# Reloading the query weight a block of heads earlier in the backward pass of an attention decode kernel

## The chip, the cores and the metric

The kernel runs on one core of a Trainium2 chip. The metric is the device time of one execution in microseconds (us); smaller is better. Before the change seven runs gave a median of 1722.65 us (1720.59 to 1726.81).

A core has a matrix engine (TensorE, PE in the profile; its weight loads are PEld), a vector engine (VectorE, DVE), a scalar engine (ScalarE, ACT), GpSimd (POOL) and SyncE (SP), which here only issues transfers. Each engine runs its own instructions in order. A DMA is issued by one of these engines and then moves on 16 DMA engines; an instruction that waits for a DMA's semaphore holds up everything behind it on its engine.

## The reference

One decode step of a pre-norm transformer block and its vector-Jacobian product: the kernel returns the output and the gradients of all inputs.

```python
def _A_ref(x, k_cache, v_cache, wq, wo):          # B=4, Sq=1, D=512, H=32, Dh=128, Sk=4096
    q = (x @ wq).reshape(B, Sq, H, Dh).transpose(0, 2, 1, 3)
    scores = jnp.einsum("bhqd,bhkd->bhqk", q, k_cache) * (Dh ** -0.5)
    p = _softmax(scores, axis=-1)
    o = jnp.einsum("bhqk,bhkd->bhqd", p, v_cache)
    return o.transpose(0, 2, 1, 3).reshape(B, Sq, H * Dh) @ wo

h  = x + _A_ref(_layernorm(x), k_cache, v_cache, wq, wo)
h2 = h + _B_ref(_layernorm(h), w1, w3, w2)         # SwiGLU, F=1792
_out, _vjp = jax.vjp(_f, A_x, A_k_cache, A_v_cache, A_wq, A_wo, B_w1, B_w3, B_w2)
return (_out, *_vjp(grad_out))
```

All arrays are bf16. There are 4 x 32 = 128 heads (batch times head); each has a key and a value cache of 4096 x 128, 1 MiB apiece, and each cache has a gradient of the same size. So 128 MiB of keys and 128 MiB of values are read, the values a second time for the backward pass, and 256 MiB of gradients are written.

## The kernel before

**Two passes over the heads.** The forward pass takes the heads in pairs: it reads K and V, computes the softmax `P_all`, and keeps for each head a small matrix M (in eight slots of 16 heads) from which the gradient of the query is later formed. A middle part runs the feed-forward block forward and backward. The backward pass is the loop at L1175, one turn per head `s`:

- `prefetch` (L1168) or L1179 issues the load of the value cache of a later head (seven are held) from ACT (L793).
- `front(s + 1)` (L1140): TensorE transposes V of the next head in four groups (L760), ACT copies each back from PSUM (L761), TensorE forms `dP` with 32 small matmuls (L1148). Every fourth head `replicate` (L1126, L1129) first rebuilds the row copies `reps` that all of VectorE's products read.
- `grad_V(s + 1)`: VectorE writes the 1 MiB gradient of V into a slot `gv` (L766), POOL issues the store (L777).
- `grad_K(s)` (L1154): VectorE turns `dP` into `dS` (L1158, L1161) and writes the 1 MiB gradient of K into a slot `gk` (L766), SP issues the store (L1165).
- a turn of side work.

**Slots.** SBUF is cut into 23 slots of about 1 MiB. `Slot(...)` takes the slot that has been free longest, `give` puts it at the end of that queue. A slot is given back when its store has been issued; the next user of the same slot waits, by semaphore, for that store to have landed. So the length of the free queue is the number of stores that can be under way. Seven slots circulate among the value loads; the rest of the free ones carry `gv`, `gk` and the side work's tiles.

**Order of the DMAs.** The instruction streams show that each load and store issued from SP or ACT takes the next of eight semaphores in turn, and is issued only when the previous user of its semaphore has landed. With one value load and one `gk` store per head, a store waits for the `gk` store of four heads before, and a value load for the value load of four heads before. One more DMA on SP, a load of the side work, shifts this by one: for the four heads after it a value load waits for a `gk` store. POOL's stores have eight semaphores of their own.

**Side work.** `side_work` (L947) is a generator. The loop advances it by one step per head from head 21 and by three steps per head from head 59 (L1190). Its order is: 128 matmuls that form the gradient of the query from the M slots, three per step, which give back an M slot after each 16 (L952 to L957); the scaling into `dqT_bf` (L959 to L965); four small POOL transfers that lay it out as `dqflat` (L969); then the gradient with respect to the layernorm output, for which the query weight `A_wq` is read again in four slices of 1 MiB (`load_wq2`, L975, issued on SP at L977). For each slice `cc` TensorE transposes 32 blocks (L992), ACT copies them back (L994), and TensorE adds 32 matmuls (L997). After the four slices come the layernorm backward and the remaining weight gradients.

In the kernel before, slice 0 is asked for in step 46 of the side work (head 61) and first used in step 52 (head 63). Slices 1, 2 and 3 are asked for in steps 50, 59 and 68 and used in steps 61, 70 and 79.

Of the kernel before, what the change touches and what calls it, by code (L numbers as in the profile page):

```python
# [24 lines left out]
def kernel(  # L25
# [22 lines left out]
    nc = tc.nc  # L48
    P = nc.NUM_PARTITIONS
# [8 lines left out]
    HD = H * Dh  # L58
    assert NH == P and Dh == P and H == 32 and Sk == 32 * P
    assert D == 4 * P and F % P == 0  # L60
    DC = D // P
# [5 lines left out]
    MC = 16  # L67
# [107 lines left out]
    def ones_window(col):  # L175
# [11 lines left out]
                          in_=rowg[:, None, :, None].to_broadcast([P, 4, 8, 4]))  # L187
# [100 lines left out]
    def M_of(s):  # L288
        return Ms[s // MC].f(MC * (Dh + 1)).rearrange("p (n c) -> p n c", c=Dh + 1)[:, s % MC, :]
# [633 lines left out]
    with ExitStack() as c2:  # L923
# [23 lines left out]
        def side_work():  # L947
            pt = psg.tile([P, Dh], BF16, tag="gps", name="pt_O")
            nc.tensor.transpose(pt[:], OT_bf[:], ident_b[:])
            nc.scalar.copy(out=O_sb[:], in_=pt[:])  # L950
            dq_ps = psx.tile([P, 512], FP32, tag="x2", name="dq_ps")
            for s in range(NH):  # L952
                nc.tensor.matmul(dq_ps[:, s:s + 1], lhsT=M_of(s)[:, 0:Dh], rhs=dOT_f[:, s:s + 1], start=True, stop=True)
                if s % MC == MC - 1:
                    Ms[s // MC].give()
                if s % 3 == 2:
                    yield  # L957
            yield
# [11 lines left out]
            yield  # L970

            dx_ps = psx.tile([P, 512], FP32, tag="x2", name="dx_ps")
            wq2s = deque()

            def load_wq2(cc):  # L975
                wq2s.append(Slot("wq2"))
                nc.sync.dma_start(out=wq2s[-1].b(HD), in_=A_wq[cc * P:(cc + 1) * P, :])  # L977

            load_wq2(0)
            for _ in range(4):  # L980
                yield
            for cc in range(DC):
                if cc + 1 < DC:
                    load_wq2(cc + 1)
                yield
                yield
                wq2 = wq2s.popleft()
                wv = wq2.b(HD).rearrange("p (n c) -> p n c", c=P)
                for h0 in range(0, H, 8):
                    pt = psg.tile([P, 8, P], BF16, tag="gps", name="pt_wq")  # L990
                    for i in range(8):
                        nc.tensor.transpose(pt[:, i, :], wv[:, h0 + i, :], ident_b[:])  # L992
                    yield
                    nc.scalar.copy(out=wv[:, h0:h0 + 8, :], in_=pt[:])  # L994
                yield
                for h in range(H):
                    nc.tensor.matmul(dx_ps[0:B, cc * P:(cc + 1) * P], lhsT=dqT_bf[:, h * B:(h + 1) * B], rhs=wv[:, h, :],  # L997
                                     start=(h == 0), stop=(h == H - 1))
                    if h == H // 2 - 1:
                        yield  # L1000
                wq2.give()
                yield
            yield
            fs = Slot("fin")
# [55 lines left out]
            for i in range(2):  # L1060
                st = Slot("gw2")
                hw = hh_rows[:, i * 7 * P:(i + 1) * 7 * P].rearrange("b (p k) -> b k p", k=7)
                for k in range(7):
# [4 lines left out]
                                  in_=st.b(7 * D).rearrange("p (c j) -> p c j", c=7))  # L1068
# [4 lines left out]
            for (rows, out_ap) in ((dg_rows, out_6), (du_rows, out_7)):  # L1073
                for i in range(2):
                    st = Slot("gw13")
                    nw = hhat_bf[0:B, i * 2 * P:(i + 1) * 2 * P].rearrange("b (p k) -> b k p", k=2)
                    for k in range(2):
                        for (f0_, w_) in f_chunks:
# [5 lines left out]
                                      in_=st.b(2 * F).rearrange("p (c f) -> p c f", c=2))  # L1084
                    st.give()
            r1.give()
            for h0 in range(0, H, 8):
                st = Slot("gwo")
                ow = oflat.b(HD)[0:B, h0 * P:(h0 + 8) * P].rearrange("b (p k) -> b k p", k=8)
                for k in range(8):  # L1090
# [4 lines left out]
                                  in_=st.b(8 * D).rearrange("p (k j) -> p k j", k=8))  # L1095
                st.give()
            oflat.give()
            r2.give()

        units["s"] = side_work()  # L1100


# [121 lines left out]
```

## Time and profile before

| what | value |
|---|---|
| median of 7 runs | 1722.65 us |
| the profiled execution, its own time | 1722.65 us |
| its span, first to last instruction | 1720.3 us |
| bytes moved by DMA | 707.86 MB, mean 411 GB/s |
| HBM read, written | 422.59 MB, 282.34 MB |
| busy: TensorE, VectorE, ScalarE, GpSimd | 77%, 73%, 56%, 23% |
| one value load, one `gv` store, one `gk` store, issue to landing (median) | 15.2, 29.0, 22.4 us |
| a reload of the query weight, issue to landing (least, median, most) | 25.3, 29.5, 34.3 us |

The time between the span and the profiled execution's own time is 2.35 us. The profile cuts the span into 40 slices of 43 us; "DMA" is the mean busy share of the 16 DMA engines and "GB/s" what they moved. "idle before, releaser" stands for the time an engine sat idle just before an instruction, and what ended it. Where a stretch is asked for, each line gives the busy time of every engine in it, the granted clock of TensorE, the DMA share and the rate.

### The profile page before, as it was taken

To read this page: it belongs to the slowest core of one execution; us is meant where nothing else is said; L and a number is where in the kernel's file an instruction comes from. 1 tells how busy PE (TensorE), PEld (TensorE's weight loads), DVE (VectorE), ACT (ScalarE), POOL (GpSimd) and SP (SyncE) were. 2 spreads that over 40 slices of the span, in tenths; PEclk is the share of its full clock that TensorE was granted. 3 is DMA by queue.
4 is the path that set the end of the run, shared out by engine and by line. 5 is a ranking of instruction groups with operands and counts; after the bars stand their busy time and mean duration, and the time that the engine had idled before them with its cause. 6 is when DMAs were issued, how large, how long until landed. Compare 5 with 4: busy or idle time off the path is not lost. (4 is left out here: it accounts for less than half of the span.)

```text
span 1720.3 us, 44172 instructions
## 1 busy us (share of the span) xinstructions
PE 1329.8 (77%) x19124; PEld 1127.9 (66%) x19124; DVE 1253.1 (73%) x1389; ACT 960.2 (56%) x1470; POOL 401.8 (23%) x689
## 2 busy tenths in 40 slices
PE   5889888888888888887888787872777768777853
PEld 4767666676666666876778777762665556555652
DVE  5989899989998997666776766653667647555575
ACT  3455444444454444676655555552676657666752
POOL 1211222222222231231322211211223122212220
PEclk9999999999999999666555555565885565565555
DMA  9999999999999999999999999999999999999996
GB/s 397 418 419 418 419 418 419 418 419 419 413 416 408 419 404 390 381 420 423 422 422 423 423 422 423 422 422 405 371 423 412 425 426 405 404 422 422 421 422 286
DMA packets 101762, 707.86 MB, mean 411 GB/s; under 512 B 11052, under 2 KB 15288, under 8 KB 17600
## 3 DMA queue, kind: packets, MB, share of 16 engines
q1 hardware_dynamic: 63568, 432.04, 61.0%
q0 software_dynamic: 20864, 148.22, 20.6%
q10 hardware_dynamic: 17136, 124.79, 17.7%
q8 instruction: 150, 2.46, 0.6%
q14 instruction: 44, 0.36, 0.1%
HBM read 422.59 MB, written 282.34 MB: 410 GB/s over the span
## 5 line engine op out<-in xcount | busy, mean ns | idle before, releaser
L761 ACT COPY V<-pt_tps 128x1024 bf16<-128x1024 bf16 x512 | 492.8, 1016 | 200.2 <-PE pt_tps L760 178.5
L760 PE MATMUL pt_tps<-ident_b,V 128*128 128x128 bf16 x4096 | 453.5, 293 | 77.4 <-ACT V L761 73.6
L760 PEld LDWEIGHTS <-V 128*128 128x128 bf16 x4096 | 402.3, 138 | 142.2 <-issue 133.9
L766 DVE TENSOR_TENSOR gv<-P,reps 128x4096 bf16<-128x4096 bf16 x125 | 287.1, 2297 | 195.4 <-ACT reps L1129 83.6
L766 DVE TENSOR_TENSOR gk<-dS,reps 128x4096 bf16<-128x4096 bf16 x128 | 294.0, 2297 | 114.9 <-DMA out_dram<-gv 82.8
L433 PE MATMUL M_ps<-PK,Vn 128*128 128x130 bf16 x4096 | 285.2, 222 | 56.1 <-DMA Vn<-in_A_v_cache_dram 55.9
L418 DVE TENSOR_TENSOR PK<-Kn,PK 128x4096 bf16<-128x4096 bf16 x128 | 292.3, 2283 | 31.2 <-POOL PK L414 30.9
L433 PEld LDWEIGHTS <-Vn 128*128 128x128 bf16 x4096 | 251.6, 99 | 77.9 <-DMA Vn<-in_A_v_cache_dram 71.2
L325 DVE STREAM_TRANSPOSE KT<-Kn 128x512 f32<-128x512 f32 (+1 forms) x321 | 250.6, 797 | 0.3 <-issue 0.2
L320 ACT COPY KT<-pt_tps 128x1024 bf16<-128x1024 bf16 x128 | 129.5, 1012 | 197.0 <-PE pt_tps L319 152.0
L777 POOL DMA_DIRECT2D out_dram<-gv x128 | 68.3, 534 | 676.9 <-DVE dSt L1158 588.1
L1148 PE MATMUL dP_ps<-dOT_bf,V 128*128 128x1 bf16 x4096 | 151.0, 166 | 81.8 <-ACT V L761 61.4
L1148 PEld LDWEIGHTS <-V 128*128 128x128 bf16 x4096 | 140.3, 103 | 95.4 <-ACT V L761 72.9
L1138 POOL COPY P<-P_all 128x64 bf16<-128x64 bf16 x125 | 144.9, 1159 | 0.0
L331 POOL TENSOR_TENSOR W<-qrep,wmask 128x128 bf16<-128x128 bf16 x128 | 122.7, 958 | 83.7 <-PE S_ps L351 69.1
L414 POOL COPY PK<-P_all 128x64 bf16<-128x64 bf16 x128 | 32.6, 255 | 420.7 <-ACT P_all L408 417.6
L408 ACT COPY P_all<-pt_P 32x64 bf16<-32x64 bf16 x256 | 52.1, 203 | 58.4 <-PE pt_P L404 56.1
L1129 ACT CAST reps<-rep_ps 128x512 bf16<-128x512 f32 x62 | 36.4, 587 | 81.1 <-PE rep_ps L1126 47.0
L319 PE MATMUL pt_tps<-ident_b,Kn 128*128 128x128 bf16 x1024 | 80.8, 224 | 0.0
L443 PE MATMUL kP_ps<-PK,onesw 128*32 128x512 bf16 x1024 | 80.1, 389 | 0.0
L319 PEld LDWEIGHTS <-Kn 128*128 128x128 bf16 x1024 | 62.2, 100 | 25.9 <-issue 25.9
L351 PE MATMUL S_ps<-KT,W 128*32 128x256 bf16 x1536 | 75.5, 286 | 0.5 <-DVE KT L325 0.2
(239 smaller groups left out, 1283.4 us busy)
## 6 DMA issues: line engine op xcount, KB each, us to landing
Kn<-in_A_k_cache_dram SPq DMA_DIRECT2D x128, 1024.0 KB, 15.6
Vn<-in_A_v_cache_dram SPq DMA_DIRECT2D x128, 1024.0 KB, 16.2
out_dram<-gv POOLq DMA_DIRECT2D x128, 1024.0 KB, 29.0
out_dram<-gk SPq DMA_DIRECT2D x128, 1024.0 KB, 22.4
V<-in_A_v_cache_dram ACTq DMA_DIRECT2D x119, 1024.0 KB, 14.6
V<-in_A_v_cache_dram SPq DMA_DIRECT2D x9, 1024.0 KB, 19.0
wq<-in_A_wq_dram SPq DMA_DIRECT2D x8, 1024.0 KB, 18.2
out_dram<-gw POOLq DMA_DIRECT2D x6, 896.0 KB, 36.6
```

Of the source, the lines that this page charges most:

```text
L319: nc.tensor.transpose(pt[:, i, :], Kn[:, c * GW + i, :], ident_b[:])
L320: nc.scalar.copy(out=KT[:, c * GW:(c + 1) * GW, :], in_=pt[:])
L325: nc.vector.transpose(out=KT[:, c * w_:(c + n) * w_], in_=Kn[:, c * w_:(c + n) * w_])
L331: nc.gpsimd.tensor_tensor(out=W[:, hl], in0=qrep[:, :, s:s + 1].to_broadcast([P, 4, 32]), in1=wmask[:, hl, None, :].to_broadcast([P, 4, 32 ...
L418: nc.vector.tensor_tensor(out=PK[:, :, 0:Dh].rearrange("p j (r t) -> p j r t", t=2), in0=Ks[s].heads().rearrange("p j (r t) -> p j r t", t=2),
L433: nc.tensor.matmul(hold["M"][:], lhsT=Vn[:, j, :], rhs=PK[:, j, :], start=(j == 0), stop=(j == SJ - 1))
L443: nc.tensor.matmul(hold["kP"][32 * q:32 * (q + 1), :, :], lhsT=ones_window(w), rhs=PK[:, j0:j0 + 4, 0:Dh], start=(w == 0 and c == 0), stop ...
L760: nc.tensor.transpose(pt[:, i, :], v[:, g * GW + i, :], ident_b[:])
L761: nc.scalar.copy(out=v[:, g * GW:(g + 1) * GW, :], in_=pt[:])
L766: nc.vector.tensor_tensor(out=dst.rearrange("p j (r t) -> p j r t", t=2), in0=col2[:, :, None, :].to_broadcast([P, SJ, Dh // 2, 2]), in1=r ...
L1138: nc.gpsimd.tensor_copy(out=P2s[s][:], in_=P_all[:, s, :, None].to_broadcast([P, SJ, 2]))
L1148: nc.tensor.matmul(dP_ps[:, j:j + 1], lhsT=VT[:, j, :], rhs=dOT_bf[:, s:s + 1], start=True, stop=True)
```

## The change

The two definitions are moved ahead of the first loop of the side work. Slice 0 is asked for when the fourth M slot has been given back, and slice 1 when the sixth has. Slices 2 and 3 are asked for when the slice two before has been used up, one step earlier in the turn of the loop than before. The four empty steps ahead of the slices are gone.

```diff
+            wq2s = deque()
+
+            def load_wq2(cc):
+                wq2s.append(Slot("wq2"))
+                nc.sync.dma_start(out=wq2s[-1].b(HD), in_=A_wq[cc * P:(cc + 1) * P, :])
+
             dq_ps = psx.tile([P, 512], FP32, tag="x2", name="dq_ps")
             for s in range(NH):
                 nc.tensor.matmul(dq_ps[:, s:s + 1], lhsT=M_of(s)[:, 0:Dh], rhs=dOT_f[:, s:s + 1], start=True, stop=True)
                 if s % MC == MC - 1:
                     Ms[s // MC].give()
+                    if s // MC in (3, 5):
+                        load_wq2(s // MC // 5)
                 if s % 3 == 2:
                     yield
@@
             dx_ps = psx.tile([P, 512], FP32, tag="x2", name="dx_ps")
-            wq2s = deque()
-
-            def load_wq2(cc):
-                wq2s.append(Slot("wq2"))
-                nc.sync.dma_start(out=wq2s[-1].b(HD), in_=A_wq[cc * P:(cc + 1) * P, :])
-
-            load_wq2(0)
-            for _ in range(4):
-                yield
             for cc in range(DC):
-                if cc + 1 < DC:
-                    load_wq2(cc + 1)
                 yield
                 yield
                 wq2 = wq2s.popleft()
@@
                 wq2.give()
+                if cc + 2 < DC:
+                    load_wq2(cc + 2)
                 yield
```

After it the four slices are asked for in steps 22 (head 42), 32 (head 52), 54 (head 64) and 63 (head 67) of the side work, and used in steps 48, 57, 66 and 75 (heads 62, 65, 68 and 71). All side work behind them comes four steps sooner.

## The prediction

> **What bounds the kernel.** I read the two rows of rates in forty slices first, then the busy time of the engines in chosen stretches of the backward pass, then the instructions in order of time where the rate drops, and last the table of waits.
>
> ```profile
> DMA  9999999999999999999999999999999999999996
> GB/s 397 418 419 418 419 418 419 418 419 419 413 416 408 419 404 390 381 420 423 422 422 423 423 422 423 422 422 405 371 423 412 425 426 405 404 422 422 421 422 286
> ```
>
> The transfers bound it: no slice but the last is under 90% busy, and in the backward pass (slice 17 on) the rate stands at 422 GB/s. No compute engine is over 77%. So a change is worth what it does to the stretches below 422. The deepest are slices 27 and 28, 405 and 371, where the query weight is read again. Cut into stretches:
>
> ```profile
> 720.00:1165.00 445.00, 356.11 (x4499) 329.51 (x4500) 303.95 (x257) 266.36 (x293) 108.81 (x128) 0.56 1.01 421
> 1165.00:1195.00 30.00, 4.89 (x68) 4.39 (x67) 12.10 (x9) 5.03 (x6) 3.97 (x8) 0.56 1.01 418
> 1195.00:1220.00 25.00, 18.18 (x255) 16.78 (x256) 7.74 (x7) 15.13 (x16) 0.77 (x2) 0.69 0.86 331
> 1228.00:1236.00 8.00, 6.84 (x96) 6.42 (x95) 7.81 (x8) 5.58 (x6) 3.71 (x4) 0.71 1.00 341
> 1236.00:1295.00 59.00, 41.88 (x646) 37.23 (x644) 37.30 (x37) 39.74 (x45) 13.38 (x15) 0.82 1.01 424
> 1295.00:1305.00 10.00, 8.28 (x99) 5.70 (x95) 9.79 (x9) 7.65 (x12) 5.92 (x5) 0.50 0.99 372
> 1425.00:1435.00 10.00, 7.72 (x106) 5.42 (x105) 9.78 (x9) 8.32 (x12) 6.29 (x6) 0.67 0.99 356
> ```
>
> From 1165 to 1195 TensorE (first busy time) works 4.89 of 30 us, yet the rate holds at 418: queued transfers cover. Then they run out: 25 us at 331, share 0.86. Later dips, 8 to 10 us at 341 to 372, have a share near 1 and a VectorE (third time) that is busy almost without a break: it catches up after a wait. The instructions say why:
>
> ```profile
> 1171.97 0.33 ACTq L793 DMA_DIRECT2D V<-in_A_v_cache_dram  x1
> 1172.37 0.34 SPq L977 DMA_DIRECT2D wq<-in_A_wq_dram  x1
> 1172.40 0.59 ACT L1129 CAST reps<-rep_ps 128x512 bf16<-128x512 f32 x1 [11.68 <-DMA V<-in_A_v_cache_dram]
> 1173.04 0.58 PE L1126 MATMUL rep_ps<-qrows_bf,ident_b 128*128 128x128 bf16 x4 [11.44 <-ACT reps L1129]
> ...
> 1197.74 1.89 PE L992 MATMUL pt_wq<-ident_b,wq 128*128 128x128 bf16 x16 [18.83 <-DMA wq<-in_A_wq_dram]
> 1198.81 1.01 ACT L994 COPY wq<-pt_wq 128x1024 bf16<-128x1024 bf16 x1 [20.31 <-PE pt_wq L992]
> 1198.87 0.33 ACTq L793 DMA_DIRECT2D V<-in_A_v_cache_dram  x1
> ...
> 1205.00 0.25 DVE L1158 TENSOR_SCALAR dSt<-dP_ps,c_rep 128x32 f32<-128x32 f32 x1 [19.64 <-PE dP_ps L1148]
> ```
>
> Slice 0 is issued at 1172.37 and first used at 1197.74, 25.4 us later; TensorE stands 18.8 us at it. Behind it on TensorE are the transposes of the next V, behind those ACT's copies and the next value load, and VectorE gets no `dP` for 19.6 us. Just before, ACT had waited 11.68 us to issue a value load: the load of slice 0 had shifted the turn of the eight semaphores, and this value load waited for a `gk` store. The two waits in a row emptied the queue; the table of waits has the second once only:
>
> ```profile
> PEld L992 <- DMA wq<-in_A_wq_dram: 18.9, 1, 18.9
> PE pt_wq L992 <- DMA wq<-in_A_wq_dram: 18.8, 1, 18.8
> ```
>
> **The change part by part.** Durations are from the profiled execution; its own time, 1722.65 us, is the median, and 2.35 us lie outside its span.
>
> *Removed: the wait for slice 0.* Slice 0 goes out 19 `gk` stores sooner on SP (43 instead of 62 ahead of it), slice 1 ten sooner (53 instead of 63). In steady state SP issues a `gk` store every 7.8 us, so slice 0 has some 20 heads or 156 us until its use and slice 1 13 heads or 101 us, against landings of 25.3 to 34.3. Both will be there. The stretch 1195 to 1220 lost (422 - 331)/422 x 25 = 5.4 us: that is the gain if the queue no longer runs out. Its bounds are 5.4 and 0, the latter if another wait empties it. I take 5.4. The dip at 1228 to 1236, where VectorE catches up, lost (422 - 341)/422 x 8 = 1.5 us, and goes with the wait.
>
> *Moved: two loads on SP at heads 42 and 52.* No instruction is added: four loads of 0.34 us issue, the same bytes. What moves with each is the shift of the semaphores: for four heads value loads wait for `gk` stores, on ACT ahead of its copies, so TensorE and VectorE behind them are late. The nearest row is the 11.68 us above. From below it costs nothing: after the loads of slices 2 and 3 in the kernel before (1209.7 and 1232.9) VectorE waits up to 9.6 us for `reps`, yet 1236 to 1295 runs at 424; and 1165 to 1172, right behind the 11.68 us, still ran at 415 or more. From above each costs one catch-up dip, 1.5 us. I take nothing: both come with a full queue and no second wait near.
>
> *Two slots held longer.* From head 42 the free queue is one shorter, from 52 two: 10 to 13 instead of 11 to 15 up to head 61. It hides: at heads 19 to 26, with 6 or 7 free, slices 18 to 21 run at 422 to 423. I take 0; the upper bound is a further dip of 1.5.
>
> *Changed: slices 2 and 3.* They are used 12 steps after they are asked for, 4 heads, instead of 11. But before, the first wait had emptied the queue and SP ran right behind VectorE. Now the queue is full. SP issues `gk` of head 61 at 1164.8, 10 us after `front(62)` ended on TensorE at 1154.6. So the lead is 4 x 7.8 to 8.3 (with the weight's extra MiB) less 10, some 21 to 23 us, and TensorE would wait 2 to 13 us for each slice, less what the semaphore shift makes TensorE late anyhow. A wait of 11.4 us cost no rate above, one of 18.8 behind it did. Bounds: 0, and 5.4 + 1.5 = 6.9 each. I take one dip of 1.5 and 1.0 of a half-emptied queue, nearer the lower end since 2 to 13 is nearer to 11.4 than to 30.
>
> *Four steps sooner.* The later side work meets other heads. Its dips (1295: 1.2 us; 1425: 1.6 us) come from waits for particular slots and may move either way, 2.8 us at most; I take 0. The side work ends at head 111 instead of 112, far from the end, which is bound by stores; nothing comes of that.
>
> Sum: -5.4 - 1.5 + 1.5 + 1.0 = -4.4; 1722.65 - 4.4 = 1718.2 us.
>
> One rule speaks against so much. The Trainium skill, DMA: Bandwidth & Descriptors, section Specifications, gives a limit of about 358 GB/s for one core's share of HBM. If that were the ceiling, 331 GB/s would be a loss of only (358 - 331)/358 x 25 = 1.9 us and the dip at 341 of 0.4, and an estimate by that page would be 1722.65 - 1.9 - 0.4 + 2.5, about no change. The measured 421 GB/s over 445 us rules it out here, where one core runs, and I go by 422.
>
> **The rivals.**
>
> *The wait only moves.* Slices 2 and 3 keep about the landing of slice 0 and a full queue; if the shift (11.7 us) and the wait for the slice fall together for one of them as before, the queue empties there: +5.4 + 1.5 against -6.9, that is 1722.7, with 1720 to 1725. For it: a lead of 21 to 23 against landings up to 34.3. Against it: the shift makes TensorE late and so gives the load more time.
>
> *Slower: both slices empty it.* One mechanism, place heads 64 to 71: each of slices 2 and 3 comes with a wait like the 18.8 us. Price 2 x 6.9 - 6.9 = +6.9, 1729.6. It decides from where shift and wait add up to about 30 us twice; then the result is over 1726. Against it: after the first such wait SP no longer lags and the second load gets its 32 us, as slices 2 and 3 did before.
>
> *More.* The later dips also go: -5.4 - 1.5 - 0.5 (398 GB/s in 1172 to 1180) - 2.8 = -10.2, 1712.5.
>
> That the change doesn't do what it says can be left out: SP's stream shows the loads moved, and nothing ahead of them on SP waits for the side work.
>
> **How the numbers follow.** Forecast (1715 to 1720.5): 0.52. The wait only moves: 0.24. Both empty it: 0.16. More: 0.08. About 0.2%, 3.4 us, is what a measurement of this kernel can tell from no change: faster is below 1719.2, slower above 1726.1. Of the forecast's 0.52 I count 0.44 as faster and 0.08 as same; with the others faster is 0.52, same 0.32, slower 0.16. The range reaches from the most that can go, 1712.5, to the edge of the slower case, 1726.0; the forecast's own range is 1715 to 1720.5.
>
> **What would show it.** Right: no wait of the transposes L992 for slices 0 and 1; no stretch near head 62 with a DMA share under 0.95; rates of 420 to 424 around heads 42 and 52 in spite of an ACT wait of some 11 us at each; the loads of slices 2 and 3 with 20 us or more to landing. Wrong: a share under 0.9 in heads 64 to 72 (the wait moved), or a dip after head 42 or 52 (the shift is not hidden).

## The result

| | before | after |
|---|---|---|
| median | 1721.5 us (1719.8 to 1726.8, 59 executions) | 1725.6 us (1722.1 to 1728.3, 23 executions) |
| ratio to before, 95% interval | | 1.0018 (1.0013 to 1.0024) |
| span of the profiled execution | 1720.3 us | 1724.4 us |

The 1722.65 us that the prediction starts from is the median of the first seven of the 59. By the ratio the change costs 3.1 us (2.2 to 4.1). That is under the 0.2% that I had named as what a measurement can tell, and yet outside the interval: a very small loss where I had forecast a gain of 4.4 us.

In the kernel after, `load_wq2` issues on L955, the transposes of a slice are L989, ACT's copies of it L991, the `reps` copies L1128, their matmuls L1125. The first two rows of the page, after:

```profile
DMA  9999999999999999999999999999999999999996
GB/s 397 418 419 418 419 418 419 418 418 418 412 417 406 419 404 391 378 421 423 424 424 425 425 426 425 425 413 409 398 366 421 424 421 410 391 421 418 420 422 277
```

The two low slices before the change (405 and 371, slices 27 and 28, the first being 0) are four now: 413, 409, 398 and 366 in slices 26 to 29. The hole is wider, not filled, and the pair at slices 33 and 34 is a little deeper (410 and 391 against 405 and 404). The waits of TensorE for the slices, after:

```profile
PE pt_wq L989 <- DMA wq<-in_A_wq_dram: 2.5, 1, 2.5
```

The three numbers are us in total, times and the longest. 18.8 us have become 2.5. So the wait that the change removes is gone. What has come in its place is seen in the stretches, after (length, busy time of PE, PEld, DVE, ACT, POOL, granted clock, DMA share, GB/s):

```profile
1015.00:1060.00 45.00, 29.62 (x364) 27.84 (x364) 26.87 (x21) 21.61 (x24) 11.03 (x10) 0.54 1.01 425
1060.00:1110.00 50.00, 36.90 (x445) 34.75 (x445) 32.41 (x28) 24.29 (x26) 9.04 (x14) 0.53 1.01 426
1125.00:1135.00 10.00, 8.78 (x117) 8.39 (x115) 9.54 (x9) 5.44 (x6) 5.11 (x5) 0.50 0.98 376
1165.00:1175.00 10.00, 8.38 (x94) 7.75 (x95) 8.73 (x10) 6.05 (x7) 5.67 (x8) 0.50 0.96 359
1205.00:1235.00 30.00, 17.30 (x242) 15.43 (x242) 16.11 (x13) 15.76 (x18) 7.71 (x6) 0.73 0.98 384
1250.00:1290.00 40.00, 30.77 (x465) 26.51 (x463) 28.62 (x31) 29.47 (x35) 12.60 (x12) 0.83 0.95 361
1455.00:1515.00 60.00, 39.33 (x428) 29.99 (x427) 31.16 (x27) 34.10 (x47) 11.80 (x20) 0.53 0.99 391
```

Against 423 GB/s each row loses (423 - rate)/423 of its length: 1.1 and 1.5 us in the two dips at 1125 and 1165, 2.8 and 5.9 us where slices 2 and 3 are issued and used, 4.5 us in the later weight gradients. The kernel before loses 5.4, 1.5 and 1.2 at the query weight (the prediction's rows) and 2.0 in the last of these stretches, which runs there at

```profile
1455.00:1515.00 60.00, 42.93 (x488) 33.01 (x488) 34.63 (x28) 38.85 (x53) 14.54 (x21) 0.59 1.01 409
```

The instructions of ACT in order of time show the shift of the semaphores after each of the four loads on SP (issued at 1015.7, 1106.4, 1202.9 and 1224.9), after:

```profile
1023.03 0.59 ACT L1128 CAST reps<-rep_ps 128x512 bf16<-128x512 f32 x1 [17.38 <-DMA out_dram<-gk]
...
1114.20 1.93 ACT L761 COPY V<-pt_tps 128x1024 bf16<-128x1024 bf16 x2 [15.23 <-DMA out_dram<-gk]
...
1210.24 1.93 ACT L761 COPY V<-pt_tps 128x1024 bf16<-128x1024 bf16 x2 [7.50 <-DMA out_dram<-gk]
...
1240.39 1.93 ACT L761 COPY V<-pt_tps 128x1024 bf16<-128x1024 bf16 x2 [4.66 <-DMA out_dram<-gk]
```

Each time a value load stands in front of ACT's copies and waits for a `gk` store. VectorE, which makes all the stores, is late behind the last two:

```profile
1218.63 2.29 DVE L766 TENSOR_TENSOR gv<-P,reps 128x4096 bf16<-128x4096 bf16 x1 [15.78 <-ACT reps L1128]
...
1244.90 0.25 DVE L1157 TENSOR_SCALAR dSt<-dP_ps,c_rep 128x32 f32<-128x32 f32 x1 [8.94 <-PE dP_ps L1147]
...
1255.55 2.29 DVE L766 TENSOR_TENSOR gv<-P,reps 128x4096 bf16<-128x4096 bf16 x1 [7.82 <-ACT reps L1128]
```

15.8 us idle, and then 16.8 of some 20. A dip goes with each (1215 to 1235 and 1250 to 1270), and in five us of the second the share falls to 0.70:

```profile
1255.00:1260.00 5.00, 4.24 (x46) 4.01 (x46) 4.38 (x4) 3.87 (x5) 1.86 (x2) 0.53 0.70 282
```

### The profile page after: what moved, and what is told of

The parts are those of the page before. It is cut to its first block, busy times and chain, and to the rows that moved or that the text cites. A ratio compares the mean times of both kernels' runs of the same rounds, so it can differ in the third digit from the quotient of the medians.

```text
span 1724.4 us, 44171 instructions
## 1 busy us (share of the span) xinstructions
PE 1330.8 (77%) x19124; PEld 1129.6 (66%) x19124; DVE 1253.7 (73%) x1389; ACT 960.7 (56%) x1470; POOL 418.6 (24%) x689
## 4 chain that ended last, share of the span: by engine, by line
DMA 44%; DVE 7%; PE 5%; ACT 3%; issue 3%; POOL 0%; ACTq 0%; DVEq 0%; SPq 0%; POOLq 0%
DMA out_dram<-gk 21%; DMA out_dram<-gv 16%; DVE gv L766 3%; DMA wq<-in_A_wq_dram 3%; DMA out_dram<-gw 2%; DMA w2b<-in_B_w_dram 2%; ACT V L761 2%; DVE gk L766 2%; PE pt_tps L760 1%; PE M_ps L433 1%; DVE PK L418 1%; PE pt_w L562 0%; POOL P L1137 0%; PE o_ps L1051 0%; ACT Pn L397 0%
## 5 line engine op out<-in xcount | busy, mean ns | idle before, releaser
L761 ACT COPY V<-pt_tps 128x1024 bf16<-128x1024 bf16 x512 | 492.6, 1015 | 218.9 <-PE pt_tps L760 174.8
L1137 POOL COPY P<-P_all 128x64 bf16<-128x64 bf16 x125 | 160.7, 1286 | 0.0
L1128 ACT CAST reps<-rep_ps 128x512 bf16<-128x512 f32 x62 | 36.4, 586 | 79.6 <-PE rep_ps L1125 59.0
L397 ACT ACTIVATE Pn<-E,rl 128x1024 bf16<-128x1024 f32 x64 | 73.7, 1152 | 3.2 <-DVE rl L394 3.2
## 6 DMA issues: line engine op xcount, KB each, us to landing
Kn<-in_A_k_cache_dram SPq DMA_DIRECT2D x128, 1024.0 KB, 15.8
wq<-in_A_wq_dram SPq DMA_DIRECT2D x8, 1024.0 KB, 20.3
```

The lines of the kernel that those rows point to most:

```text
L761: nc.scalar.copy(out=v[:, g * GW:(g + 1) * GW, :], in_=pt[:])
L1137: nc.gpsimd.tensor_copy(out=P2s[s][:], in_=P_all[:, s, :, None].to_broadcast([P, SJ, 2]))
```

## The experiments

The first three theories: **A**, the shift of the semaphores that each lone load on SP brings is no longer hidden when two come near each other; **B**, the two slots held from heads 42 and 52 are missing; **C**, the later side work, four steps sooner, meets worse heads. **D**, that time not lost at the query weight is lost at the next late transfer, came with the first results; **E** and **F** are given where they came up.

For each run I cut the profiled execution into stretches of 5 us and add up (423 - rate)/423 x 5. "Heads 49 to 54" is 1100 to 1185 us, "query weight" 1185 to 1310, "row stage" 1340 to 1530 (the row copies, their matmuls and the weight gradients that follow); these three columns add up only the stretches under 412 GB/s, the column "700 to 1700" adds up all. The ratio is that of the measured times, to the kernel before on the same chip; the losses are those of one execution.

| run | median, us | ratio (95%) | heads 49-54 | query weight | row stage | 700 to 1700 | span |
|---|---|---|---|---|---|---|---|
| before | 1721.5 | | 0.4 | 8.1 | 3.8 | 17.4 | 1720.3 |
| after | 1725.6 | 1.0018 (1.0013-1.0024) | 2.6 | 8.4 | 4.8 | 20.4 | 1724.4 |
| 1 all from POOL | 1724.2 | 1.0012 (1.0003-1.0021) | 0.5 | 6.5 | 8.4 | 20.1 | 1723.7 |
| 2 in pairs | 1723.5 | 1.0006 (0.9997-1.0015) | 3.1 | 0.5 | 8.3 | 17.9 | 1720.8 |
| 3 slices 0, 1 from POOL | 1722.0 | 0.9998 (0.9989-1.0006) | 0.3 | 1.4 | 11.1 | 18.2 | 1721.3 |
| 4 slices 2, 3 from POOL | 1723.3 | 1.0007 (0.9998-1.0016) | 2.8 | 0.7 | 10.2 | 17.5 | 1721.0 |
| 5 empty steps back | 1722.5 | 1.0004 (0.9995-1.0013) | 1.5 | 9.2 | 1.5 | 17.3 | 1720.8 |
| 6 = 3 with 5 | 1721.1 | 0.9992 (0.9983-1.0001) | 0.0 | 0.2 | 9.8 | 15.4 | 1718.0 |
| 7 before, lone shifts | 1722.2 | 1.0003 (0.9994-1.0012) | 0.0 | 9.5 | 2.5 | 15.5 | 1719.5 |
| 8 before, slots held | 1722.9 | 1.0003 (0.9994-1.0012) | 0.5 | 8.3 | 1.9 | 17.2 | 1721.0 |
| 9 = 6, rows early | 1721.1 | 0.9996 (0.9987-1.0005) | 0.3 | 0.6 | 11.3 | 16.6 | 1719.0 |
| 10 = 9, oflat early | 1721.2 | 0.9995 (0.9986-1.0004) | 1.0 | 0.4 | 6.0 | 15.8 | 1719.1 |
| 11 before, rows early | 1722.9 | 1.0008 (0.9999-1.0016) | 0.0 | 10.1 | 2.0 | 19.6 | 1723.7 |
| 12 before, close shifts | 1723.0 | 1.0005 (0.9996-1.0013) | 0.0 | 7.6 | 3.5 | 18.1 | 1722.3 |
| 13 after, two steps | 1727.5 | 1.0030 (1.0018-1.0042) | 2.3 | 7.6 | 3.7 | 19.4 | 1723.7 |
| 14 after, four steps | 1722.7 | 1.0005 (0.9996-1.0014) | 1.9 | 7.7 | 7.5 | 21.9 | 1723.0 |
| 15 = 6, two steps at rows | 1721.2 | 0.9989 (0.9980-0.9998) | 0.0 | 0.2 | 12.5 | 16.7 | 1718.4 |
| 16 before, two steps | 1724.3 | 1.0014 (1.0005-1.0022) | 0.0 | 8.3 | 6.0 | 20.1 | 1725.6 |
| 17 = 9, row slots kept | 1722.5 | 1.0000 (0.9991-1.0009) | 0.5 | 1.1 | 11.2 | 17.4 | 1719.4 |
| 18 = 10, row slots kept | 1721.5 | 0.9997 (0.9988-1.0005) | 1.3 | 0.9 | 7.0 | 16.9 | 1720.1 |

Over these 20 executions the span rises by 1.09 us for each us of the column "700 to 1700" (correlation 0.89): the account of lost transfer explains most of the differences in span. The single columns do not stand for it (correlations 0.23, 0.65 and -0.39), and this is what the rest is about.

A rate under 423 is not the same as idle DMA engines. Between 1165 and 1530 us the engines' missing share, (1.01 - share) x 5 us over the same stretches, adds up to 4.9 us of the 12.4 lost before, 4.9 of 14.7 after and 6.4 of 10.0 in run 6. The rest is lost while the engines count as busy, as in 1455 to 1515 of the kernel after (391 GB/s at a share of 0.99); no run shows why.

### Where the slices are issued (1 to 4)

**1: all four slices from POOL**, whose stores have semaphores of their own, so that nothing shifts on SP and ACT.

```diff
-                nc.sync.dma_start(out=wq2s[-1].b(HD), in_=A_wq[cc * P:(cc + 1) * P, :])
+                nc.gpsimd.dma_start(out=wq2s[-1].b(HD), in_=A_wq[cc * P:(cc + 1) * P, :])
```

> The changed kernel with all four reloads issued from POOL instead of SP, at the same steps and into the same slots. POOL's stores have their own eight semaphores, so the turn of the eight that SP and ACT share is not shifted. Theory A, the shift of the turn is what costs: the ACT waits of 17.4 and 15.2 us for a gk store at heads 42 and 52 and the one of 7.5 us at head 65 go, the stretches below 400 GB/s between heads 52 and 72 go with them (1.1 + 1.5 + 2.7 + 5.8 = 11.1 us lost in the changed kernel), and the time falls to 1713 to 1719 us, below the kernel before (1721.5). Theory B, the two slots held early shorten the queue of stores: same slots, so the time stays at 1724 to 1727. Theory C, the later side work meets other heads four steps sooner: same steps, so it stays at 1724 to 1727.

Slower than before by 0.12%, and not in theory A's range. The dips at heads 49 to 54 are gone, but now one of the late slices is not there in time and TensorE waits 19.0 us for it, in this run's table of waits:

```profile
PE pt_wq L989 <- DMA wq<-in_A_wq_dram: 19.2, 2, 19.0
```

So this run trades the shift for the wait and does not tell them apart at slices 2 and 3.

**2: in pairs on SP**, slices 0 and 1 at head 36, 2 and 3 at head 52. Two loads in a row move the turn by two, and value loads wait for value loads again.

```diff
-                    if s // MC in (3, 5):
-                        load_wq2(s // MC // 5)
+                    if s // MC in (2, 5):
+                        load_wq2(2 * (s // MC == 5))
+                        load_wq2(2 * (s // MC == 5) + 1)
...
-                if cc + 2 < DC:
-                    load_wq2(cc + 2)
```

> The changed kernel with the four reloads still on SP but in two pairs: slices 0 and 1 when the third M slot is given back (head 36), slices 2 and 3 when the sixth is (head 52). A pair moves the turn of the eight semaphores by two, so value loads go on waiting for value loads and gk stores for gk stores. Four slots are held until use instead of two. Theory A (shift): no ACT wait for a gk store of over 5 us near heads 36, 52 and 64 to 68; time 1713 to 1719 us. Theory B (slots): four slots fewer hurt more than two, 1727 us or more. Theory C (steps): 1724 to 1727.

The query weight now loses 0.5 us instead of 8.4. But ACT waited 42.1 us for slices (two value loads had one ahead of them in the turn), heads 49 to 54 lose 3.1, and the row stage 8.3. The time is that of before within its interval, and in none of the three ranges.

**3 and 4: two slices from POOL, two from SP.**

```diff
+                (nc.gpsimd if cc < 2 else nc.sync).dma_start(out=wq2s[-1].b(HD), in_=A_wq[cc * P:(cc + 1) * P, :])
```

> The changed kernel with slices 0 and 1 issued from POOL and slices 2 and 3 from SP as they are: the shifts at heads 42 and 52 go, those at heads 64 and 67 stay. If the shifts at 42 and 52 carry the loss, the time falls to 1719 us or less. If those at 64 and 67, where 2.7 + 5.8 us are lost in the changed kernel, carry it, the time stays near 1723 to 1725.

```diff
+                (nc.sync if cc < 2 else nc.gpsimd).dma_start(out=wq2s[-1].b(HD), in_=A_wq[cc * P:(cc + 1) * P, :])
```

> The changed kernel with slices 2 and 3 issued from POOL and slices 0 and 1 from SP as they are: the shifts at heads 64 and 67 go, those at 42 and 52 stay. If the shifts at 64 and 67 carry the loss, the time falls by some 5 to 8 us, to 1717 to 1720. If those at 42 and 52 do, it stays at 1724 to 1726. By theory A the gains of this run and of the one with slices 0 and 1 on POOL add up to that of all four on POOL.

These two place the dips. With slices 0 and 1 on SP (run 4) the dips at 1125 and 1165 are there as in the kernel after; with these two on POOL (run 3) they are not. Stretches of run 4, then of run 3:

```profile
1125.00:1135.00 10.00, 8.78 (x116) 8.39 (x114) 9.54 (x9) 5.27 (x6) 5.11 (x5) 0.50 0.99 374
1165.00:1175.00 10.00, 8.38 (x95) 7.75 (x95) 8.99 (x10) 6.07 (x8) 5.80 (x8) 0.50 0.96 365
1205.00:1235.00 30.00, 21.70 (x344) 19.11 (x343) 19.73 (x16) 21.04 (x24) 6.63 (x9) 0.84 1.01 423
...
1385.00:1410.00 25.00, 12.77 (x144) 8.73 (x142) 19.10 (x17) 9.18 (x11) 8.58 (x8) 0.64 0.86 322
```

```profile
1125.00:1135.00 10.00, 7.59 (x86) 7.04 (x85) 7.37 (x6) 5.03 (x6) 2.96 (x3) 0.50 1.00 421
1165.00:1175.00 10.00, 8.05 (x127) 7.40 (x125) 6.93 (x5) 7.08 (x8) 3.88 (x6) 0.67 1.01 407
1205.00:1235.00 30.00, 20.67 (x279) 18.56 (x278) 16.12 (x14) 17.49 (x20) 9.28 (x9) 0.72 1.01 421
```

So the 2.6 us at heads 49 to 54 come from the early loads on SP. The 8.4 us at the query weight fall to 0.7 when the late pair leaves SP, and to 1.4 when the early pair does: it takes all four, one by one, to lose them. And both runs lose 10 to 11 us at the row stage, where the kernels before and after lose 4 to 5; run 4's 25 us at 322 GB/s are a hole that neither of those has. This is where theory D comes from. In time, neither run is in a range that was given for it, but both are faster than the kernel after (1.0018): run 3 by 0.0020, plus or minus 0.0010, or 3.4 us, and run 4 by 0.0011, plus or minus 0.0011, or 1.9 us, just at its bound (the half widths of the two intervals added in squares, here and below). So the early pair on SP costs time in the kernel after; without it the time is that of the kernel before, and no better.

### The four steps, alone and together with POOL (5 and 6)

```diff
+            for _ in range(4):
+                yield
```

> The changed kernel with the four empty steps put back ahead of the slices: the loads of slices 0 and 1 stay early on SP, but slices are used in steps 52, 61, 70 and 79 as in the kernel before, and all later side work meets the same heads as before. Theory C (the side work four steps sooner is what costs after head 72): the loss behind 1300 us falls from 5.2 us in the changed kernel to the 5.0 of the kernel before or less and the time is 1 to 3 us below the changed kernel's 1725.6. Theory A (shift of the turn): the shifts at heads 42, 52, 65 and 68 all stay, 1724 to 1726. Theory D (the queue of transfers that reaches the later side work full loses there what was won earlier, wherever its steps fall): 1721 to 1725, with the loss behind 1300 us larger than before.

The changed kernel with the four empty steps ahead of the slices is as fast as the kernel before within its interval: 1.0004. Against the kernel after (1.0018) that is 0.0014 or 2.4 us, plus or minus 1.8 by the two intervals (0.00055 and 0.0009 added in squares). So C holds in part. The place is the later stretch, 1455 to 1515, at 411 GB/s here against 391:

```profile
1455.00:1515.00 60.00, 41.54 (x512) 32.94 (x509) 35.69 (x29) 39.82 (x54) 15.53 (x21) 0.66 1.01 411
```

At the query weight this run loses 9.2 us, no less than the kernel after, although its table of waits has no wait of TensorE for a slice at all.

Run 6 has both: slices 0 and 1 from POOL as in run 3, and the four steps.

> Slices 0 and 1 early from POOL (no shift at heads 42 and 52, as in the run with slices 0 and 1 on POOL, which lost only 1.7 us up to 1300 but 11.1 us behind it), and the four empty steps put back. Theory C: behind 1300 us the loss is that of the kernel before, 5.0 us, so the time is some 6 us below that run's 1722.0: 1715 to 1718. Theory D: behind 1300 us it loses 9 to 11 us again in spite of the old steps, 1720 to 1723.

Its stretches show a query weight that costs nothing, and a row stage that does:

```profile
1165.00:1205.00 40.00, 28.37 (x420) 26.32 (x421) 28.79 (x24) 25.45 (x29) 11.77 (x14) 0.69 1.01 420
1205.00:1290.00 85.00, 59.83 (x854) 53.41 (x854) 55.84 (x53) 53.60 (x62) 21.86 (x25) 0.72 1.01 421
1290.00:1380.00 90.00, 68.28 (x776) 53.86 (x775) 47.76 (x40) 62.80 (x82) 19.07 (x24) 0.58 1.01 423
1385.00:1435.00 50.00, 31.55 (x350) 22.54 (x350) 33.60 (x30) 26.08 (x34) 17.07 (x18) 0.60 0.88 341
```

In 1205 to 1290, where the kernels before and after lose most of their 8 us, it runs at 421. It reaches the row stage at 423, and then loses (423 - 341)/423 x 50 = 9.7 us in one place. Its instructions there:

```profile
1375.19 0.53 POOL L1033 DMA_DIRECT2D rows<-in_grad_out_dram  x1
1384.46 0.60 POOL L1034 CAST rows<-reps 4x512 bf16<-4x512 f32 x1 [8.73 <-DMA out_dram<-gv]
```

```profile
1412.18 1.01 PE L942 MATMUL gps<-rows 4*128 4x512 bf16 x2 [11.02 <-DMA rows<-in_grad_out_dram]
```

A load of 4 KB, the rows of the output gradient, takes 36.9 us from issue to landing behind the stores on POOL's queue, and TensorE stands 11 us at it. And POOL's first write into the slot of the rows waits 8.7 us for the store that was in that slot. The kernel before has no such wait at the row slots, the kernel after one of 2.5 us on VectorE. Both have lost some 8 us shortly before, so that fewer stores may be under way; that is a reading. Both causes are tried below.

Runs 3, 5 and 6 make a table of two by two with the kernel after. The early pair on SP instead of POOL costs 0.0012 (plus or minus 0.0013) with the four steps and 0.0020 (0.0010) without; leaving out the four steps costs 0.0006 (0.0012) with the pair on POOL and 0.0014 (0.0011) with it on SP. With both undone, 1.4 us (0.0008; -0.2 to 2.9 us) are gained on the kernel before, which is no resolved difference.

### Shifts and slots by themselves (7, 8 and 12), on the kernel before

Run 7 puts two loads of 128 bytes into SP's stream, at heads 30 and 40; run 12 puts them at heads 30 and 33. Run 8 withholds one slot from head 42 and one more from head 52, both up to head 61.

```diff
+        tiny = [const.tile([1, 64], BF16, name=f"tiny{i}") for i in range(2)]
...
+            for i, at in enumerate((30, 40)):          # run 12: (30, 33)
+                if s == at:
+                    nc.sync.dma_start(out=tiny[i][:], in_=A_wq[i:i + 1, 0:64])
```

> The kernel before with two extra loads of 128 bytes on SP, one at head 30 and one at head 40. Nothing else is added or moved, so this is the shift of the turn alone, twice, in a full queue. Theory A in the strong form (each shift loses 1 to 3 us of transfer time): 1723 to 1727, with ACT waits of 11 to 17 us for a gk store behind each. In the weak form (the queue covers a lone shift): ACT waits of that length, no stretch under 400 GB/s near heads 30 to 45, and a time of 1721 to 1722.5.

> The kernel before with two loads of 128 bytes on SP at heads 30 and 33, so that the turn of the semaphores is shifted for three heads, with no slot held and nothing else moved. Theory A in its strong form (two shifts close together empty a full queue): a new dip of 2 to 5 us within 60 us of head 30's end, 1724 to 1727. Rival (the shifts near heads 64 and 67 cost only as the queue was already short there, from the slices' own loads and the side work's due transfers): no share under 410 GB/s between 900 and 1040, 1721.5 to 1723.

```diff
+            held = []
...
+                    if s // MC in (3, 5):
+                        held.append(Slot("held"))
...
+            for sl in held:
+                sl.give()
```

> The kernel before with one slot taken out of the free queue at head 42 and a second at head 52, both given back when slice 0 is asked for at head 61; nothing is loaded into them. This is the shorter queue of stores alone. Theory B (slots): 1723 us or more. Otherwise 1721 to 1722.5, as before.

B falls: run 8 has the time of before. In run 7 ACT waits 13.8 us behind the first shift and 5.9 behind the second, and no dip follows. In run 12 it waits 10.9 and 4.4 us within 31 us, as much as near heads 64 and 67 in the kernel after, and nothing is lost either:

```profile
929.89 0.58 ACT L1129 CAST reps<-rep_ps 128x512 bf16<-128x512 f32 x1 [10.93 <-DMA out_dram<-gk]
...
960.45 0.58 ACT L1129 CAST reps<-rep_ps 128x512 bf16<-128x512 f32 x1 [4.43 <-DMA out_dram<-gk]
```

```profile
900.00:940.00 40.00, 27.41 (x312) 25.84 (x311) 28.37 (x24) 17.92 (x20) 9.27 (x12) 0.50 1.01 422
940.00:980.00 40.00, 32.93 (x398) 31.07 (x397) 27.76 (x22) 22.95 (x25) 14.88 (x13) 0.50 1.01 421
980.00:1020.00 40.00, 34.29 (x404) 32.29 (x405) 25.80 (x23) 23.42 (x26) 9.14 (x10) 0.54 1.01 422
```

So A falls in its strong form. Two close shifts do not by themselves lower the rate at heads 30 to 40 of the kernel before; those of the kernel after come with losses at heads 49 to 54 and 64 to 71. What differs there is more than the pace of the side work (see runs 13 to 16): the slices' own bytes, and the slots that they hold.

### The late rows, and their slots (9 to 11, 17 and 18)

Run 9 is run 6 with the 4 KB load in the first step of the side work; run 11 is the kernel before with the same edit. Run 10 is run 9 with the slot `oflat` and its four transfers moved there too. To make room, two other small rows move by 256 columns.

```diff
+            gr_bf = rs.t[0:B, 3584:3584 + D]
+            nc.gpsimd.dma_start(out=gr_bf, in_=g2)
+            yield                                   # run 10 alone: this and the next three
+            oflat = Slot("oflat")
+            for b in range(B):
+                nc.gpsimd.dma_start(out=oflat.b(HD)[b:b + 1, :], in_=O_sb[b::B, :])
...
-            gr_bf, dh_bf, hhat_bf = r1.t[0:B, 2 * F:2 * F + D], r2.t[0:B, F:F + D], r2.t[0:B, F + D:F + 2 * D]
-            nc.gpsimd.dma_start(out=gr_bf, in_=g2)
+            dh_bf, hhat_bf = r2.t[0:B, F:F + D], r2.t[0:B, F + D:F + 2 * D]
```

> As the run with slices 0 and 1 issued early from POOL and the four empty steps put back (1721.07 us), and with the 4 KB load of the output gradient's rows moved from the row stage to the first step of the side work. Theory D (what the wq stage no longer loses is lost at the next late load, the 4 KB one): its 9.6 us at 1385 to 1435 fall to 0 to 3 and TensorE's wait for these rows to 0; 1712.5 to 1717. Rival (the queue drains there whatever is late, as the stores of a whole block come at once): the dips stay or move by less than 50 us, 1719.5 to 1722.

> As the run before it, with the slot of the output-projection's rows and its four transfers also moved to the first steps of the side work. Theory D: what the run before loses between 1440 and 1515 goes too; 0.5 to 3 us less than that run. Rival (a slot held from the start of the side work costs more than the late transfers): 1 to 5 us more than that run, with new dips before 1300.

> The kernel before with only the 4 KB load of the output gradient's rows moved to the first step of the side work. Theory D: takes away its dip of 1.9 us at 1420 to 1435 alone, 1719.0 to 1721.0, and the 6.57 us wait of TensorE for these rows; the wq stage still loses 5.4 + 1.5. Rival (this load has nothing to do with the lost time): 1721.5 to 1722.5, the dip still there.

The wait of TensorE for these rows is gone in all three, and no run is faster for it. Run 9 still loses 8.3 us at 1385 to 1420; run 11 loses its dip at 1420 (0.6 us instead of 1.9) and is, if anything, slower. Waits of run 9 at the row copies, and its rate there:

```profile
POOL rows L1035 <- DMA out_dram<-gv: 8.8, 1, 8.8
...
DVE rows L1036 <- DMA out_dram<-gv: 4.8, 1, 4.8
ACT rows L1044 <- DMA out_dram<-gv: 4.6, 1, 4.6
```

```profile
1385.00:1420.00 35.00, 22.77 (x242) 15.65 (x242) 24.62 (x22) 18.37 (x23) 12.18 (x12) 0.60 0.83 323
```

So runs 17 and 18, formed on 9 and 10, keep the two slots that the gradient before leaves, instead of giving them back and taking two whose stores are still under way. Theory **F** says that the stretch loses its 8 us or more whatever single wait is taken away, and that the waits only choose the place.

```diff
-            flat.give()
-            fs.give()
-
-            r1, r2 = Slot("rows1"), Slot("rows2")
+            r1, r2 = flat, fs
```

> The run with slices 0 and 1 early from POOL, the four empty steps and the early load of the output gradient's rows (1721.12 us), whose row stage now keeps the two slots that the weight gradient before it leaves, instead of giving them back and taking two whose stores are still in the queue. Theory D: POOL's 8.8 us, VectorE's 4.8 and ScalarE's 4.6 of waits for stores at the row stage go, and of its 8.3 us at 1385 to 1420 at most 3 stay; 1712.5 to 1717. Theory F (the stretch from 1165 to 1515 loses 8 us or more whatever single wait is taken away; the place only is chosen by the waits): the waits go, the loss stays or comes up elsewhere in that stretch; 1719.5 to 1722.

> As the run before it, with the slot of the output-projection's rows and its four transfers at the first steps of the side work too, so that none of the late things named so far is left. Theory D: 1711 to 1716. Theory F: 1719 to 1722, with 5 us or more lost between 1165 and 1515.

The waits for stores at the row copies are gone, and the time is that of before (1.0000 and 0.9997). D's ranges are missed by 5 us and more; run 18 lies in F's range, run 17 (1722.5) just above it. In run 17 the hole has moved on:

```profile
1400.00:1420.00 20.00, 11.34 (x133) 9.17 (x131) 13.52 (x13) 11.43 (x15) 3.87 (x6) 0.50 0.89 337
1435.00:1500.00 65.00, 46.14 (x496) 35.23 (x495) 42.41 (x34) 40.34 (x55) 17.02 (x23) 0.53 0.97 379
```

4.1 and 6.8 us there, 11.2 in the whole row stage against 11.3 in run 9. D, as a sum of single waits each with its own price, falls.

### The pace of the side work (13 to 16)

Theory **E**: three steps a head make the heads of this stretch longer than their transfers, so that the loss is set by the pace. Run 13 (on the kernel after) and run 16 (on the kernel before) make two steps a head for the heads 59 to 72, run 14 makes four from head 59 on, run 15 is run 6 with two steps for the heads 74 to 87.

```diff
-                step("s", 1 if s < S0 + 38 else 3)
+                step("s", 1 if s < S0 + 38 else 2 if s < S0 + 52 else 3)             # 13, 16
+                step("s", 1 if s < S0 + 38 else 4)                                   # 14
+                step("s", 1 if s < S0 + 38 else 2 if S0 + 53 <= s < S0 + 67 else 3)  # 15
```

> The changed kernel with two steps of side work a head instead of three in the 14 heads 59 to 72; the 14 steps left over follow behind. Theory E (between 1190 and 1305 the heads with three steps each take longer than their transfers, so that what is lost is set by the pace, wherever the single waits fall): the 8.4 us that the changed kernel loses between 1215 and 1290 fall to 4 or less; 1717 to 1722, or, if the later stage takes it over, that stage's 4.5 us rise by as much. Theory D (single late things, each at its own price): the dips stay within 2 us of 8.4, only later; 1724 to 1727.

> The changed kernel with four steps of side work a head instead of three from head 59 on. Theory E: the loss between 1165 and 1515, 14.5 us in the changed kernel, rises by 5 to 20 us; 1729 to 1745. Theory D: the same waits for the same things, 1723 to 1728.

> Slices 0 and 1 early from POOL and the four empty steps, as in the run of 1721.07 us, with two steps of side work a head instead of three in the 14 heads 74 to 87, where the row stage lies. Theory E: its 9.6 us at 1385 to 1435 fall to 5 or less; 1714 to 1718. Theory D (the first writes to the row stage's slots wait for stores, at their own price): 8 to 11 us there, 1719.5 to 1722.5.

> The kernel before with two steps of side work a head instead of three in the heads 59 to 72. Theory E: its 8.1 us between 1195 and 1305 fall to 4 or less, 1716 to 1720. Theory D: the wait for slice 0 shrinks by the 10 us or so that the four empty steps now cover more, so 5.4 us fall to 2 to 4 and the rest stays, 1718.5 to 1721. By both it gains; only with the run of the changed kernel does it tell them apart.

E falls: with fewer steps no kernel is faster. Run 16 is slower than before (1.0014); run 13 at 1.0030 is not told from the kernel after (0.0012, plus or minus 0.0013). With four steps the kernel after is, at 1.0005, better than with three (0.0013, plus or minus 0.0011), against E's sign. The losses at the query weight stay at 7.6, 8.3 and 7.7 us. I had expected a gain of run 16 by either theory, and it lost. Run 15 is the one kernel that is faster than before beyond its interval, by 0.11% (0.02 to 0.20); its row stage does not lose less for it than run 6's, so I do not claim that the two steps did it. Against the kernel after it is 0.29% faster.

## Why the prediction was wrong

**"Removed: the wait for slice 0", 5.4 and 1.5 us: right as to the wait, wrong as to the gain.** The wait went from 18.8 us to 2.5, slices 0 and 1 are there in time, and 1195 to 1220 no longer holds a wait for a slice. But I took the transfer lost at a wait for time that is won when the wait goes. Runs 2, 3, 4, 6, 9, 10, 15, 17 and 18 lose 0.2 to 1.4 us at the query weight, 6.7 or more less than before, and none of them is more than 0.11% or 2 us faster by its ratio; the row stage takes 6 to 12.5 us in them instead of 3.8. The clearest is run 6: 0.2 us lost at the query weight, 9.8 at the row stage, and 1.4 us (-0.2 to 2.9) gained where the sum had 6.9. That is the first step that failed. The bound of 0 that I gave, "if another wait empties it", was the right end; my rivals only looked for that wait near by, at slices 2 and 3.

**"Moved: two loads", taken at nothing: 2.6 us by place, 3.4 (plus or minus 1.7) by run 3.** This is the second step that failed. The waits of ACT came (17.4 and 15.2 us), and 1015 to 1110 ran at 425 and 426 as I had said. The catch-up came later, at 1125 and 1165: 1.1 and 1.5 us, inside the upper bound of 1.5 each. Runs 3 and 4 show that these two loads cause them, and run 3 against the kernel after that they cost time. The row that I had gone by, 11.68 us of ACT, was misread twice. It names a value load, not a `gk` store, as what ended the wait: the load issued at 1171.97 takes the semaphore of the value load issued at 1141.09, whose landing the trace has at 1171.88. So it was no price of waiting for a store. And 1165 to 1172 lies inside this wait, not behind it; the 8 us that follow ran at 398, which my own rival "More" used.

**"Two slots held longer", nothing: right.** Run 8.

**"Changed: slices 2 and 3", 1.5 + 1.0: measured 8.4 by place, and by another mechanism.** I feared a wait for the slices; that is 2.5 us. The loss comes where ACT stands 7.5 and 4.7 us behind the two shifts and VectorE 15.8 and 16.8 us behind ACT and TensorE. I had written that the shift "makes TensorE late anyhow" as a relief for the load; here the loss comes with it. With the sign I had named for it, a share under 0.9 in heads 64 to 72, the profile says so (0.70 in 1255 to 1260). It is no cost of two close shifts wherever they fall (run 12), and no wait for a slice is needed for it (run 5). Moving two of the four loads takes the loss off this place (runs 3 and 4), but the row stage takes most of it over.

**"Four steps sooner", nothing within 2.8: 2.4 (plus or minus 1.8).** The bound held; the value did not, and this is the third step that failed: with the four steps back (run 5) the change costs 0.04%, no resolved difference.

Put together: of the 6.9 us that the largest terms counted, run 6 has 1.4, which is not told from nothing; and the two terms taken at nothing, the early loads on SP and the four missing steps, turn this into the loss of 3.1. Undoing either of them alone brings the time back to that of before (runs 3 and 5). But so do other edits: the pairs (run 2), slices 2 and 3 from POOL (run 4) and four steps a head (run 14) each take 1.9 to 2.2 us off the kernel after, at or just beyond plus or minus 1.8. So the runs do not single out one cause of the loss. Of the cases that I priced, "the wait only moves" is nearest in kind, by another wait than it named.

**What stays open.** Between 1165 and 1530 us all these kernels lose 7.4 to 16.4 us, 10 to 15 in most. None of these alone carries it: the wait for the weight, the shifts, two held slots, the 4 KB load, the slots of the rows, the number of steps a head. Each was taken away, changed or (the shifts and the held slots) added by itself, and the time stayed within 0.3% of before. Lowest are runs 10 and 18 with the early `oflat` (7.4 and 9.4 us), which lose a part of it elsewhere and are not faster than runs 9 and 6. Why so much of it is kept is not shown. One reading, not tried, is that a kernel that comes to the next stage with a full queue finds more stores ahead of whatever it needs there, as the waits of runs 6 and 9 at the row slots suggest, which a kernel whose queue has just run dry does not meet.

## What to carry to other kernels

In this kernel, bound by transfers, a dip in the rate behind a wait was an upper bound of what the wait's removal could bring, not an estimate; before counting such a dip, look at what the next stages wait for and lose once the wait is gone. When loads are moved, the queue that issues them and the steps that go with them (here four empty ones) deserve runs of their own: either, undone alone, took the loss away here. And a row that is to price a term should be read for what ended its wait, not only for how long it was. Last, a profile of one execution shows where time is lost, but when the losses move, only the sum over the whole stretch compares kernels.

## What the runs showed of the hardware

- A 4 KB load on POOL's queue took 28.7 to 43.6 us from issue to landing in the fifteen kernels that issue it at the row stage, while 1 MiB stores were under way, and 20.3 to 21.2 in the five that issue it at the start of the side work; the same rows, loaded as 8 KB at the start of run 6, landed in 5.9 us. The Trainium skill, DMA: Bandwidth & Descriptors, section "Anatomy of one DMA — SWDGE (gpsimd) path", fits a DMA from GpSimd with about 2.0 us fixed plus its bytes over 436 GB/s; under this load the measurement is far above it. That the difference is time spent behind what is already queued is a reading; the order of the three cases fits it.
- At a steady 421 GB/s or more, ACT stood 10 to 17 us behind a shifted semaphore without loss of rate: 13.8 (run 7), 10.9 and 4.4 within 31 us (run 12), 17.4 (after, with 425 GB/s over 1015 to 1060). It is no rule: behind the next wait of the kernel after, 15.2 us, come the dips at 1125 and 1165.
- A load of the same 1 MiB slice that is issued on POOL instead of SP can be late by as much as the wait it was to replace: 19.0 us at TensorE in run 1, though only 6.1 in run 4.
